# A fused recurrence and wave-MLP kernel: the same steps replayed in another order

## The chip, the core and the metric

The kernel runs on one core of a Trainium2 chip. A time is the device time of one execution in microseconds (us); lower is better. Five engines work side by side: TensorE (PE in the profile; its weight loads are listed as PEld), VectorE (DVE), ScalarE (ACT), GpSimd (POOL) and SyncE (SP), which here only issues transfers. Each engine takes its own instructions strictly in the order in which the program gives them, so an instruction that waits holds up all that stand behind it on that engine.

## The reference

Two stages in a row. The first is a linear recurrence over 768 tokens, for 4 batches and 8 heads of 64 columns:

```python
gamma = 1.0 - 2.0 ** (-5.0 - np.arange(H)); scale = 1.0 / np.sqrt(D)
for t in range(S):
    state = gamma[None, :, None, None] * state + einsum('bhd,bhe->bhde', k[:, :, t], v[:, :, t])
    y[:, :, t] = scale * einsum('bhd,bhde->bhe', q[:, :, t], state)
```

Its output, laid out as x of shape (4, 768, 512), goes through

```python
theta = x @ w_theta
zr, zi = x * np.cos(theta), x * np.sin(theta)
y = einsum('ts,bsd->btd', w_tok_r, zr) + einsum('ts,bsd->btd', w_tok_i, zi)
u = x + y
out = u + np.maximum(u @ w_ch, 0.0)
```

## The kernel before

The whole kernel is a set of small functions, one for each step, and a list of tokens, ORDER, which replays them: a token names a function and its arguments (`M.3.2` calls `M(3, 2)`), and a last letter p, v, a or s names the engine or the queue (POOL, DVE, ACT, SP). Nothing else schedules: ORDER is the program's order on every engine and on every transfer queue.

**The recurrence** is cut into 24 units: 4 batches, 3 stretches of 256 tokens, 2 halves of 4 heads. For unit n:

- `Lk`, `Lq`, `Lv` load 256 KB of k, q and v each, on the queue of SP or of ACT (tiles kqf and vf; 16 and 9 buffers). `ck`, `cq` or `cqs` and `cv` cast and scale them to bf16 (tiles kqb and vb).
- `Tk` and `Tq` transpose kqb on PE into kq_ps, and `E` copies that to kqT; for some units `Tk6`, `Tq6` and `E6` do so in 64-blocks, or `Dk` does it by a transposing transfer on SP's queue.
- `A` multiplies k by q (at_ps), `m` masks the product on DVE (at), `Y` multiplies by v into r_ps. `ST` makes the unit's contribution to the state, `S0` and `S1` add it up (s), `SB` casts the state (sbd), `I` multiplies it by q into r_ps.
- `XB` and `XA` bring r_ps to the transposed output xT of a 128-token tile C.

at_ps has one buffer: `A` of the next unit waits for `m`.

**The second stage** has 24 tiles of 128 tokens, six to a batch. `Hh` multiplies xT by w_theta (th_ps, four products of 512 columns), `CN` takes cosine and sine on ACT (cs), `Tx` and `Ex` or `Dx` bring x back to token rows (x_sb), `z` multiplies them (z). The two token matrices come in by `Pw` on POOL's queue (tile row; `Pth` and `Pch` bring wth and wch) and are transposed by `Tw` and copied by `Ew` (wtr, wti). `M(t, s0)` is two of the twelve 512-column products of output tile t (y_ps); `u` adds x on DVE; `Tu` and `Eu` or `Du` transpose; `O` is four products with w_ch (o_ps); `f` makes the output on DVE, and `SO` stores it. The last tile is done in halves (`Mh`, `uh`, `Oh`, `fh`, `SOh`).

th_ps, y_ps and o_ps share a pool of two banks, acc, which are given out in turn: a group that opens waits until the group two before it has been read, which is `CN` for th_ps, `u` for y_ps and `f` for o_ps. kq_ps, x_ps, w_ps and u_ps share two other banks in the same way.

`Z` issues two products of a zero tile whose result nobody reads; its number has no effect. `const1` clears the zero tile on DVE, `const2` makes positions and decays on POOL and arg on DVE, `const3` (ACT) the scales of q and v, `constA` (POOL), `const8` and `const9` (ACT) the decay table qx, `const4` the identity and `const5` the mask on POOL, `const6` clears sbd.

Of the kernel before, what the change touches and what calls it, by code (L numbers as in the profile page):

```python
# [24 lines left out]
cqs.1.p Tq.1 Lq.2.s S0.0.v SB.0.1.v A.0 Lk.2.s SB.0.0.p cv.1.p Lv.2.s S1.0 Z.15 I.0 Z.27 m.0 Tk.1 E.1.a  # L25
cqs.2.v Z.34 cv.2.p Y.0 ST.1 XB.0.1.a S0.1.v S1.1 SB.1.0.a Pth Lq.3.s Z.18 XB.0.0.v Tq.2 A.1 SB.1.1.a
ck.2.a I.1 m.1 Y.1 ST.2 Tk.2 const7 Z.23 XB.1.0.v Lk.3.s E.2.v XB.1.1.v A.2 ck.3.p S0.2.v m.2 S1.2
SB.2.1.a Z.11 cqs.3.p Tq.3 Lv.3.s Tx.0 Tk.3 Z.3 ck.4.p Lv.4.s Lk.5.s Lq.5.s Lv.5.s Lq.6.s Lk.6.s Lv.6.s
Lq.7.s E.3.a SB.2.0.v I.2 Y.2 XB.2.1.a Ex.0.a cv.3.v cq.4.p Tk.4 Lq.8.s A.3 ST.3 Lk.7.s S0.3.v SB.3.0.a
S1.3 Lv.7.s Lk.8.s Tx.1 Tq.4 SB.3.1.p cv.4.p m.3 Pw.1.0 XB.2.0.a Ex.1.a I.3 Lv.8.s E.4.a ck.5.a cq.5.a  # L30
Y.3 Pw.0.0 ST.4 Hh.0 S0.4.v XB.3.0.v XB.3.1.v cv.5.v CN.0.1 A.4 CN.0.0 Tq.5 Hh.1 Tk.5 SB.4.0.p SB.4.1.a
Pw.0.1 Hh.2 m.4 E.5.v I.4 Y.4 ST.5 ck.6.a Tk.6 Tx.2 cq.6.a CN.1.1 CN.1.0 XA.4.1 A.5 XA.4.0 m.5 Lq.9.s
Ex.2.v S0.5.v z.0.p Tq.6 E.6.a CN.2.0 cv.6.p Hh.3 SB.5.0.v Tx.3 Tw.1.0 z.1.v SB.5.1.a Ew.1.0.v Ex.3.a
CN.2.1 A.6 I.5 Y.5 ST.6 XA.5.0 z.2.v Tw.0.0 CN.3.0 Tx.4 CN.3.1 Ew.0.0.v S0.6.v XA.5.1 Ex.4.v Hh.4 CN.4.0
CN.4.1 Tw.0.1 M.0.1 Pw.1.1 z.3.v M.0.0 Tw.0.2 Pw.1.2 Ew.0.2.a SB.6.1.a Hh.5 z.4.p SB.6.0.p Lk.9.a M.0.3
ck.7.p cqs.7.p M.0.2 CN.5.1 CN.5.0 cq.8.v m.6 Ew.0.1.v Tw.1.1 Tw.1.2 Ew.1.1.v Lv.9.s M.0.4 M.1.0 Tx.5
Ew.1.2.v M.1.1 S1.6 Tk.7 M.1.4 Pch Ex.5.v z.5.v cv.7.v Tq.8 Tq.7 M.1.2 E.7.a M.0.5 I.6 Y.6 ST.7 A.7
ck.8.a u.0 S0.7.v m.7 XA.6.1 SB.7.1.a M.1.5 M.1.3 XA.6.0 Tw.1.3 M.2.5 Pw.0.2 M.2.3 u.1 S1.7 Tk.8 M.2.1
M.2.0 SB.7.0.v Ew.1.3.a Tu.0 I.7 cv.8.v E.8.a Lk.10.s cv.9.p Y.7 ST.8 A.8 cqs.9.v ck.9.v M.2.4 Du.1
Eu.0.a XB.7.1.a XB.7.0.v S0.8.v SB.8.0.v M.2.2 Tx.6 Tq.9 Tk.9 Lv.10.a ck.10.p cv.10.p Lq.10.s S1.8 u.2  # L40
m.8 O.0 E.9.a SB.8.1.a Hh.6 Tw.1.4 I.8 Y.8 A.9 CN.6.0 Du.2 Lq.14.s CN.6.1 Ex.6.v f.0 ST.9 Tw.0.3 Hh.7
Ew.1.4.v Ew.0.3.a S0.9.v Tw.0.4 M.3.0 CN.7.0 CN.7.1 M.3.2 Dx.7 M.3.1 M.3.5 M.3.3 Lv.11.s Lk.11.s XA.8.1
Ew.0.4.v Lq.11.s M.3.4 S1.9 u.3 Tw.0.5 Tk.10 M.4.5 cqs.10.p XA.8.0 m.9 M.4.3 Tq.10 SB.9.1.a SB.9.0.a I.9
O.2 Lq.12.s Lk.12.s E.10.a Lk.15.s Ew.0.5.v Lk.14.s Y.9 ST.10 Tw6.1.5 Ew6.1.5.0.a Ew6.1.5.1.a A.10 z.7.p
# [36 lines left out]
Du.18 O.19 M.21.0 M.21.3 M.20.2 Mh.1.2 Mh.1.0 Mh.1.4 u.22 O.18 Mh.1.3 SO.15.a f.19 M.20.0 M.20.1 Tuh.0
u.21 Du.22 Du.21 f.18 M.20.3 Euh.0 M.20.4 Mh.1.1 M.20.5 u.20 O.22 Mh.1.5 uh.1 f.22 Tu.20 SO.14.a SO.19.s
Eu.20.a O.21 SO.18.a Tuh.1 Euh.1 f.21 Oa.0 Oa.1 fa.0 fa.1 Oh.0 Oh.1 SO.21.a SO.22.s SO.20.s fh.0 SOh.0
fh.1 SOh.1 Z.31
""".split()


# [618 lines left out]
```

## Time and profile before

| | |
|---|---|
| time, median of 3 runs (lowest, highest) | 164.74 us (164.14, 164.97) |
| span of the profiled execution, first to last instruction | 163.3 us |
| PE busy | 154.7 us, 95% (2100 matmuls) |
| DVE busy | 114.5 us, 70% |
| ACT busy | 78.8 us, 48% |
| POOL busy | 74.3 us, 45% |
| moved by DMA | 35.19 MB, mean 215 GB/s |
| chain that ended last | PE 79%, DMA 7%, DVE 6%, POOL 4% |

The profile is one execution; its own time is not listed beside its span, and the median of the timed runs is 1.4 us longer than that span. Shares are over the whole span, which hides that the first 33 us differ from the rest: the views by stretch tell them apart. A matmul's busy time includes its passage through the array, so products that follow each other closely overlap in it; the distance between their starts is what they cost.

### The profile page before, as it was taken

To read this page: it belongs to the slowest core of one execution; us is meant where nothing else is said; L and a number is where in the kernel's file an instruction comes from. 1 tells how busy PE (TensorE), PEld (TensorE's weight loads), DVE (VectorE), ACT (ScalarE), POOL (GpSimd) and SP (SyncE) were. 2 spreads that over 40 slices of the span, in tenths; PEclk is the share of its full clock that TensorE was granted. 3 is DMA by queue.
4 is the path that set the end of the run, shared out by engine and by line. 5 is a ranking of instruction groups with operands and counts; after the bars stand their busy time and mean duration, and the time that the engine had idled before them with its cause. 6 is when DMAs were issued, how large, how long until landed. Compare 5 with 4: busy or idle time off the path is not lost.

```text
span 163.3 us, 5070 instructions
## 1 busy us (share of the span) xinstructions
PE 154.7 (95%) x2100; PEld 85.5 (52%) x2100; DVE 114.5 (70%) x217; ACT 78.8 (48%) x147; POOL 74.3 (45%) x106
## 2 busy tenths in 40 slices
PE   5996989999999998999999999999999999999992
PEld 1454646656666654644544655455545554444561
DVE  3388687987994786794999787698867760345362
ACT  4966698983658264673423645822341616000020
POOL 7657289176514770520057689910469204600000
PEclk9999999999999999999999999999999999999999
DMA  4999999999999999999999999999896527514446
GB/s 116 297 290 252 258 294 240 277 220 285 226 162 275 296 205 220 251 207 245 335 236 172 242 195 305 222 192 276 185 251 129 101 64 225 161 68 128 128 156 230
DMA packets 70118, 35.19 MB, mean 215 GB/s; under 512 B 27472, under 2 KB 67152, under 8 KB 70096
## 3 DMA queue, kind: packets, MB, share of 16 engines
q1 hardware_dynamic: 57088, 24.00, 68.6%
q10 hardware_dynamic: 10320, 7.47, 16.6%
q0 software_dynamic: 2688, 3.41, 12.1%
q8 instruction: 16, 0.26, 0.7%
q14 instruction: 6, 0.05, 0.1%
HBM read 25.69 MB, written 6.29 MB: 196 GB/s over the span
## 4 chain that ended last, share of the span: by engine, by line
PE 79%; DMA 7%; DVE 6%; POOL 4%; issue 1%; ACT 1%; DVEq 0%; POOLq 0%
PE y_ps L559 33%; PE o_ps L595 10%; PE th_ps L511 10%; PE zz L279 5%; PE r_ps L458 4%; PE at_ps L380 4%; DMA x_sb<-xT 4%; DMA kqT<-kqb 3%; PE kq_ps L318 3%; PE w_ps L533 2%; DVE at L389 2%; POOL z L525 2%; PE r_ps L446 2%; PE y_ps L620 2%; PE r_ps L408 1%
## 5 line engine op out<-in xcount | busy, mean ns | idle before, releaser
L559 PE MATMUL y_ps<-z,wtr 128*128 128x512 bf16 x138 | 52.4, 380 | 0.0
L559 PE MATMUL y_ps<-z,wti 128*128 128x512 bf16 x138 | 52.3, 379 | 0.0
L525 POOL TENSOR_TENSOR z<-cs,x_sb 128x1024 bf16<-128x1024 bf16 x12 | 25.5, 2135 | 17.7 <-ACT cs L518 10.8
L389 DVE TENSOR_TENSOR at<-at_ps,mask 128x1024 bf16<-128x1024 f32 x24 | 29.2, 1215 | 0.5 <-PE at_ps L380 0.5
L310 POOL TENSOR_TENSOR vb<-vf,vsc 128x512 bf16<-128x512 f32 x15 | 15.6, 1045 | 21.7 <-ACT sbd L136 11.7
L601 DVE SCALAR_TENSOR_TENSOR ot<-o_ps,u 128x512 f32<-128x512 f32 x22 | 15.1, 688 | 13.6 <-PE o_ps L595 13.5
L511 PE MATMUL th_ps<-wth,xT 128*128 128x512 bf16 x96 | 24.5, 380 | 0.0
L566 DVE TENSOR_TENSOR u<-y_ps,x_sb 128x512 bf16<-128x512 f32 x23 | 15.8, 688 | 10.9 <-PE y_ps L559 10.5
L595 PE MATMUL o_ps<-wch,uT 128*128 128x512 bf16 x88 | 22.6, 380 | 0.0
L518 ACT ACTIVATE cs<-th_ps,halfpi 128x512 bf16<-128x512 f32 x24 | 16.3, 682 | 11.8 <-PE th_ps L511 7.0
L518 ACT ACTIVATE cs<-th_ps,zerob 128x512 bf16<-128x512 f32 x24 | 16.4, 684 | 10.6 <-PE th_ps L511 5.1
L559 PEld LDWEIGHTS <-wtr 128*128 128x128 bf16 x138 | 13.5, 98 | 13.4
L559 PEld LDWEIGHTS <-wti 128*128 128x128 bf16 x138 | 13.5, 98 | 12.7 <-issue 0.4
L138 POOL CAST sbd<-s 64x256 bf16<-64x256 f32 (+1 forms) x20 | 8.4, 418 | 24.3 <-DVE s L426 22.1
L136 ACT COPY kqT<-kq_ps 128x1024 bf16<-128x1024 bf16 (+1 forms) x10 | 9.7, 969 | 9.8 <-PE kq_ps L318 9.5
L511 PEld LDWEIGHTS <-xT 128*128 128x128 bf16 x96 | 8.7, 98 | 8.5
L279 PE MATMUL zz<-zero 128*128 128x512 bf16 x30 | 10.8, 495 | 1.9 <-DVE zero L191 1.9
L595 PEld LDWEIGHTS <-uT 128*128 128x128 bf16 x88 | 8.1, 98 | 8.4 <-issue 0.2
L136 ACT CAST kqb<-kqf 128x512 bf16<-128x512 f32 x16 | 9.6, 620 | 5.5 <-DMA kqf<-in_k_dram 5.4
L458 PE MATMUL r_ps<-at,vb 64*64 64x128 bf16 x384 | 10.0, 221 | 1.6 <-DVE at L389 1.6
L380 PE MATMUL at_ps<-kqT 64*64 64x128 bf16 x384 | 10.0, 220 | 1.1 <-DVE kqT L138 0.6
L476 DVE TENSOR_TENSOR xT<-r_ps,qx 128x256 bf16<-128x256 f32 x22 | 8.7, 417 | 1.8 <-PE r_ps L458 0.8
(88 smaller groups left out, 209.4 us busy)
## 6 DMA issues: line engine op xcount, KB each, us to landing
vf<-in_v_dram SPq DMA_DIRECT2D x20, 256.0 KB, 5.7
kqf<-in_k_dram SPq DMA_DIRECT2D x19, 256.0 KB, 5.4
kqf<-in_q_dram SPq DMA_DIRECT2D x17, 256.0 KB, 5.7
out_dram<-ot ACTq DMA_DIRECT2D x12, 256.0 KB, 2.5
out_dram<-ot SPq DMA_DIRECT2D x11, 256.0 KB, 2.4
kqf<-in_q_dram ACTq DMA_DIRECT2D x7, 256.0 KB, 5.4
kqf<-in_k_dram ACTq DMA_DIRECT2D x5, 256.0 KB, 6.7
vf<-in_v_dram ACTq DMA_DIRECT2D x4, 256.0 KB, 5.7
```

Source lines behind the costliest of these rows:

```text
L136: nc.scalar.copy(dst, src)
L279: nc.tensor.matmul(t[:m, :cols], K["zero"][:, :m], K["zero"][:, :cols], start=True, stop=True)
L310: engines[e].tensor_mul(in_blocks(vb), by_token(raw["vf", n]), _bcast_last(K["vsc"][:, i, :, h * HU:(h + 1) * HU], D))
L380: nc.tensor.matmul(at_ps[cols, g, j, a, :], kq_at(n, 0, a, j, c)[rows], kq_at(n, 1, slice(0, 2), j, c)[rows], start=(j == 0 and a == 0), s ...
L389: nc.vector.tensor_mul(at.rearrange("p g j a t -> p (g j) (a t)"), st["at_ps", n].rearrange("p g j a t -> p (g j) (a t)"), _bcast_mid(K["m ...
L458: nc.tensor.matmul(st["R", n + 1][c][g * D:(g + 1) * D, j * P:(j + 1) * P], st["vb", n][rows, lo:lo + D], st["at", n][rows, g, j, a, :], s ...
L511: nc.tensor.matmul(th_ps, st["xT", C][:, j, :], K["wth"][:, j, :], start=(j == 0), stop=(j == 3))
L518: nc.scalar.activation(st["cs", C][:, w, :], st["th_ps", C], AF.Sin, bias=K["zerob" if w else "halfpi"], scale=1.0)
L525: engines[e].tensor_mul(st["z", b][:, c], st["cs", C], _bcast_mid(x_of(C), 2))
L559: nc.tensor.matmul(st["y", t], K["wT"][r][:, s0, t0 * P:(t0 + 1) * P], st["z", b][:, s0, r, :], start=(done == 0 and r == 0), stop=(done = ...
L566: nc.vector.tensor_add(st["u", t], st["y", t], st["x", b][:, t0, :])
L595: nc.tensor.matmul(o_ps, st["uT", t][:, j, :], K["wch"][:, j, :], start=(j == 0), stop=(j == nD - 1))
```

## The change

Only ORDER is replaced, one table of tokens by another. Nearly all its lines differ, so the diff says little by itself; its first and last lines are

```diff
-const2 Lv.0.s const1 const6.v Z.29 Z.2 const5 Z.38 Lk.0.a const3 Z.35 Z.8 Lq.0.s Lv.1.s Z.28 constA
-const4 Lq.1.a const9 Lk.1.s Z.39 const8 ck.0.p Tk.0 ck.1.a cqs.0.v cv.0.v Tq.0 E.0.v Lq.4.a ST.0 Lk.4.a
...
+const1 Lq.1.a Z.472 const6.v Z.617 Lv.0.s constA Z.838 const2 const4 Lk.1.s Lk.0.a Z.896 Lq.0.s const3
+Z.362 cqs.1.v Lv.1.s ck.0.p Tk.0 const9 cv.0.v ck.1.p Z.692 ST.0 Lq.4.a cqs.0.v S0.0.a Tq.1 S1.0 Tq.0
...
-fh.1 SOh.1 Z.31
+Euh.1 Oa.1 fa.0 Oh.0 Oh.1 fa.1 SO.21.s fh.0 SO.20.s fh.1 SOh.0 SOh.1 Z.31
```

Of the 936 tokens before, 928 are left: the eight that go are `Z`, of which 15 become 7 (30 zero products become 14). Before, seven stand ahead of `Tk.0`, seven among units 0 to 3, one at the end; now five ahead of `Tk.0`, one behind it, one at the end. All other steps are there once as before. Another engine has 128 of the casts, copies and scalings, and 9 of the stores another queue (four from ACT's to SP's, five the other way). The rest is order. As the file is one line shorter, line numbers in the rows of the changed kernel are smaller by one.

Place 1, ACT at the very start. kqf is a load; qsc and vsc are `const3`; qx of 512 columns is `const9` and of 256 is `const8`; kqT<-kq_ps is `E`; s<-r_ps is `S0`; the cast kqb<-kqf is `ck.1`. Before:

```order
L156 DMA kqf<-in_k_dram 128x4x128
L239 ACT_TABLE_LOAD
L239 ACTIVATE qsc<-arg,lscale 128x48
L239 ACTIVATE vsc<-arg,zerob 128x48
L156 DMA kqf<-in_q_dram 128x4x128
L232 ACTIVATE qx<-pos,lscale,lgp 128x512 x4
L232 ACTIVATE qx<-pos,lscale,lgp 128x256 x4
L136 CAST kqb<-kqf 128x512
L156 DMA kqf<-in_q_dram 128x4x128
L156 DMA kqf<-in_k_dram 128x4x128
L136 COPY kqT<-kq_ps 128x1024
```

Now:

```order
L155 DMA kqf<-in_q_dram 128x4x128
L155 DMA kqf<-in_k_dram 128x4x128
L238 ACT_TABLE_LOAD
L238 ACTIVATE qsc<-arg,lscale 128x48
L238 ACTIVATE vsc<-arg,zerob 128x48
L231 ACTIVATE qx<-pos,lscale,lgp 128x512 x4
L155 DMA kqf<-in_q_dram 128x4x128
L135 COPY s_199<-r_ps 128x128
L155 DMA kqf<-in_k_dram 128x4x128
L135 COPY kqT<-kq_ps 128x1024
L231 ACTIVATE qx<-pos,lscale,lgp 128x256 x4
```

The k of unit 0 is now the second load of ACT's queue. The copy to kqT is now that of unit 0 (before, of unit 1; unit 0 had it on DVE), behind the large half of the qx table and two loads, and ahead of the small half.

Place 2, POOL at the start, from the positions on. pos and lgp are `constA`, posn to zerob `const2`, mask `const5`, kqb `ck`, the sbd casts `SB`. Before:

```order
L204 IOTA posn 128x6
L208 MEMSET lg 128x1 x8
L210 MEMSET lscale 128x1
L212 MEMSET halfpi 128x1
L214 MEMSET zerob 128x1
L260 MEMSET mask 128x256
L264 AFFINE_SELECT mask<-mask 64x128 x4
L222 IOTA pos 128x768
L227 MEMSET lgp 64x1 x8
masks.py:197 MEMSET ident 128x128
masks.py:199 AFFINE_SELECT ident<-ident 128x128
L138 CAST kqb<-kqf 128x512
```

Now, from the positions of `const2` on (pos and lgp stand ahead of these rows):

```order
L203 IOTA posn 128x6
L207 MEMSET lg 128x1 x8
L209 MEMSET lscale 128x1
L211 MEMSET halfpi 128x1
L213 MEMSET zerob 128x1
masks.py:197 MEMSET ident 128x128
masks.py:199 AFFINE_SELECT ident<-ident 128x128
L137 CAST kqb<-kqf 128x512 x2
L137 CAST sbd_74<-s_199 64x2x64
L259 MEMSET mask 128x256
L263 AFFINE_SELECT mask<-mask 64x128 x4
L137 CAST sbd_74<-s_199 64x2x64
```

The mask has moved from the front to behind two casts and an `SB`, which waits for unit 0's state; pos and lgp have moved ahead of what arg needs.

Place 3, PE at the end of output tile 8, where the th_ps group of tile 13 opens (`M` of tile 8, then `Hh.13`). With buffer numbers; y_ps_1976 and y_ps_1869 are tile 8's bank. Before:

```order
L559 LDWEIGHTS wtr_101
L559 MATMUL y_ps_1976<-z_1427,wtr_101 128x512
L559 LDWEIGHTS wti_102
L559 MATMUL y_ps_1976<-z_1427,wti_102 128x512
L511 LDWEIGHTS xT_1972
L511 MATMUL th_ps_2064<-wth_99,xT_1972 128x512
```

Now:

```order
L558 LDWEIGHTS wtr_80
L558 MATMUL y_ps_1869<-z_1458,wtr_80 128x512
L558 LDWEIGHTS wti_81
L558 MATMUL y_ps_1869<-z_1458,wti_81 128x512
L510 LDWEIGHTS xT_1945
L510 MATMUL th_ps_2029<-wth_78,xT_1945 128x512
```

The rows look alike, but the bank differs. Before, tile 8 opened its bank after `O.5`, so `Hh.13` takes the bank of `O.5`, and the one that takes tile 8's is the group behind it, that of `M.10.1`. Now tile 8 opens before `O.5`, so `Hh.13` itself takes tile 8's bank and waits for `u.8`.

More of the change, by code (lines that the diff above doesn't have):

```diff
@@ L28 @@
[L28 to L32, printed above, removed]
@@ new lines @@
+M.11.4 M.11.1 SB.17.0.a Lk.19.s ck.22.v SB.17.1.a CN.15.1 XA.16.0 M.11.2 ck.21.v XA.16.1 m.17 CN.15.0
+I.17 Hh.14 u.11 Y.17 Ex.15.a z.12.p ST.18 Eu6.8.0.v CN.14.0 XA.17.1 S0.18.a XA.17.0 CN.14.1 S1.18
+SB.18.1.p Dx.14 Tu6.11 A.18 SB.18.0.a z.15.v O.10 ck.19.a Eu6.11.1.v Eu6.11.0.a z.14.p Hh.17 f.10
+CN.17.1 Tq.19 Lq.23.s m.18 I.18 SO.7.s Tk.19 CN.17.0 cv.19.p O.8 E.19.v Hh.16 SO.1.s CN.16.1 f.8 Lq.22.a
+A.19 Tx6.17 Y.18 ST.19 Lv.23.s O.11 CN.16.0 M.13.0 Ex6.17.1.a Dx.16 M.13.2 z.16.p m.19 M.13.3 f.11
@@ L85 @@
+Euh.0 O.22 Mh.1.4 SO.18.a SO.19.a Tu.20 f.22 Mh.1.3 Mh.1.5 O.21 SO.22.s Eu.20.a uh.1 Tuh.1 Oa.0 f.21
+Euh.1 Oa.1 fa.0 Oh.0 Oh.1 fa.1 SO.21.s fh.0 SO.20.s fh.1 SOh.0 SOh.1 Z.31
 """.split()
```

106 lines of the change are left out of this document (52 added, 54 removed).

## The prediction

> **What bounds the kernel now.** I read the page first, for the engine that has no room.
>
> ```profile
> span 163.3 us, 5070 instructions
> PE 154.7 (95%) x2100; PEld 85.5 (52%) x2100; DVE 114.5 (70%) x217; ACT 78.8 (48%) x147; POOL 74.3 (45%) x106
> PE   5996989999999998999999999999999999999992
> DMA  4999999999999999999999999999896527514446
> ```
>
> PE is busy for 95% of the span. Busy is no proof of full use, so next come the stretches, cut at the first th_ps product, the first y_ps product and the last one of the kernel (us, then busy time and count of PE, PEld, DVE, ACT, POOL, the granted clock, the DMA share and GB/s).
>
> ```profile
> 7.82:22.15 14.33, 11.49 (x275) 7.79 (x274) 10.74 (x21) 9.88 (x20) 8.41 (x12) 1.00 1.19 271
> 22.15:32.70 10.55, 10.31 (x183) 6.54 (x179) 9.13 (x19) 9.68 (x18) 6.31 (x8) 1.00 1.17 266
> 32.70:64.00 31.30, 31.30 (x423) 18.45 (x420) 24.96 (x49) 18.61 (x32) 16.98 (x16) 1.00 1.16 237
> 64.00:104.00 40.00, 39.35 (x682) 21.39 (x682) 32.87 (x60) 19.74 (x44) 20.66 (x22) 1.00 1.19 247
> 104.00:159.80 55.80, 55.80 (x534) 29.12 (x533) 33.29 (x60) 15.17 (x29) 16.66 (x17) 1.00 0.69 159
> 159.80:163.30 3.50, 0.58 (x4) 0.08 (x1) 0.60 (x2) 0.00 (x0) 0.00 (x0) 1.00 0.61 217
> ```
>
> From 32.70 to 159.80, that is 127.1 us, PE sits idle for 0.65 us (the 64 to 104 row: 40.00 less 39.35). Those products all stay. So the time is the moment of the first y_ps product, plus 127.1, plus whatever PE waits more or less than 0.65 us in between, plus a tail of 3.5 us. The order can win in the first 32.7 us, where PE is idle by 2.84 us and 0.24 us in two rows and also computes zeros, and it can lose anywhere.
>
> The 0.65 us has two places, from the timeline:
>
> ```profile
> 64.90 0.42 PE L380 MATMUL at_ps<-kqT 64*64 64x128 bf16 x16 [0.49 <-DMA kqT<-kqb]
> 103.05 0.45 PE L318 MATMUL kq_ps<-ident,kqb 128*128 128x128 bf16 x5 [0.16 <-POOL kqb L138]
> ```
>
> **The head, part by part.** The rows of the timeline on which the walk rests (start, duration, what; in brackets the engine's idle time ahead and who ended it):
>
> ```profile
> 1.38 0.21 DVE L216 TENSOR_TENSOR arg<-posn,lg 128x48 f32<-128x48 f32 x1 [1.38 <-POOL lscale L210]
> 1.59 0.27 DVE L191 MEMSET zero<- 128x256 uint32 x1
> 1.67 1.28 ACT L239 ACT_TABLE_LOAD   x1 [1.67 <-DVE arg L216]
> 1.92 6.06 PE L279 MATMUL zz<-zero 128*128 128x512 bf16 x14 [1.92 <-DVE zero L191]
> 2.96 0.78 POOL L222 IOTA pos<- 128x768 f32 x1
> 3.68 1.07 POOL L227 MEMSET lgp<- 64x1 f32 x8
> 3.96 4.89 ACT L232 ACTIVATE qx<-pos,lscale,lgp 128x512 f32<-128x512 f32 x8 [0.43 <-POOL lgp L227]
> 5.33 0.61 POOL L138 CAST kqb<-kqf 128x512 bf16<-128x512 f32 x1
> 6.07 0.69 DVE L304 TENSOR_TENSOR kqb<-kqf,qsc 128x512 bf16<-128x512 f32 x1 [3.11 <-DMA kqf<-in_q_dram]
> 7.18 1.08 POOL L304 TENSOR_TENSOR kqb<-kqf,qsc 128x512 bf16<-128x512 f32 x1 [1.24 <-DMA kqf<-in_q_dram]
> 7.82 0.61 PE L318 MATMUL kq_ps<-ident,kqb 128*128 128x128 bf16 x8
> 8.46 0.69 DVE L138 COPY kqT<-kq_ps 128x1024 bf16<-128x1024 bf16 x1 [1.10 <-PE kq_ps L318]
> 9.18 0.53 ACTq L156 DMA_DIRECT2D kqf<-in_k_dram  x1
> 9.21 0.42 PE L380 MATMUL at_ps<-kqT 64*64 64x128 bf16 x16 [0.21 <-DVE kqT L138]
> 10.97 1.01 ACT L136 COPY kqT<-kq_ps 128x1024 bf16<-128x1024 bf16 x1 [1.61 <-PE kq_ps L318]
> ```
>
> *Zero products.* Of the chain of waits, one row gives their later price, and the fourteen first ones above give the early one, 6.06/14 = 0.43 us each:
>
> ```profile
> 10.28 0.43 PE zz L279 x2
> ```
>
> So each is 0.43 us at first and 0.216 us later. The zero tile's clearing no longer waits behind arg, so they start some 0.5 us earlier, near 1.3, and ten of them end near 5.6. The six pairs that go from units 0 to 3 were 6 x 0.43 = 2.6 us of PE; they stood where the next real step was late anyway, so by themselves I cost them at nothing, and what they hid is walked through next.
>
> *Unit 0.* The second load of a kind that was asked for lands about 6.0 (the scaling at 6.07 starts on it) and the fourth about 7.1 (the one at 7.18). k of unit 0 is now second on its queue, so it lands between these, its cast of 0.61 follows, and the first transpose stands near 7.2, against 7.82. Then it loses: arg waits for pos and lgp, 1.8 us of POOL, so the table load starts near 3.6, the scales end near 5.4, the large half of qx (four of eight in 4.89 us, the longer ones, some 2.9) ends near 8.3. Behind it come a load (0.5), the state copy, another load (0.53) and only then unit 0's kqT, at 1.01 on ACT against 0.69 on DVE: done near 10.5, where it was done at 9.15. The product of k and q follows, 1.3 us later than at 9.21. The mask, now behind an `SB` on POOL, is done near 11.1 and no later than that product.
>
> *Units 1 to 5.* The mask products are the beat of this stretch:
>
> ```profile
> 13.00 1.22 DVE L389 TENSOR_TENSOR at<-at_ps,mask 128x1024 bf16<-128x1024 f32 x1
> 20.41 1.21 DVE L389 TENSOR_TENSOR at<-at_ps,mask 128x1024 bf16<-128x1024 f32 x1
> 26.99 0.42 PE L380 MATMUL at_ps<-kqT 64*64 64x128 bf16 x16
> 29.07 0.50 PE L533 MATMUL w_ps<-ident,row 128*128 128x128 bf16 x6
> 32.70 0.38 PE L559 MATMUL y_ps<-z,wtr 128*128 128x512 bf16 x1
> ```
>
> I walked the new order by hand with these durations, each step starting at the last of its inputs and of its engine. `E.1` now stands on DVE behind `m.0`, so `m.1` is at 13.5 (13.00 before). `ck.2` and `SB.1.0` stand on ACT behind the small half of qx, which delays `Y.1` by 1.3 us, but `Tk.2` and `Tk.3` stand ahead of `Y.1` now and not behind it, so `E.2` runs during the wait: `m.3` near 21.0 (20.41). There `Hh.0` and `Hh.1`, 1.7 us of real products, stand ahead of `Y.3` and fill its wait. Unit 5's product of k and q comes near 26.4 (26.99), and the first y_ps product near 32.1 (32.70): **-0.6 us**. The error of such a walk is some 1 us on either side; the bounds for the first y_ps product are 31.0, if `E.0` and the loads come at the early end, and 33.6.
>
> *Casts elsewhere.* By means from the costliest groups, kept apart by shape:
>
> ```profile
> L136 ACT COPY kqT<-kq_ps 128x1024 bf16<-128x1024 bf16 x9 | 9.1, 1011 | 9.5 <-PE kq_ps L318 9.5
> L138 DVE COPY kqT<-kq_ps 128x1024 bf16<-128x1024 bf16 x3 | 2.1, 688 | 1.2 <-PE kq_ps L318 1.1
> ```
>
> Net five such copies go from ACT to DVE: +3.4 us there and -5.1 here. Counting all 128 with the means of their groups, DVE gains about 1 us, ACT loses 4, POOL gains 0.5. After 32.70 PE hides that: DVE has 36 us of room there. Without that cover the price would be DVE's 1 us. Cost: nothing.
>
> **The middle.** Here I looked for places where PE's next step has too little PE work ahead of it to cover its chain. One stands out, place 3: `Hh.13` takes the bank of tile 8 and waits for `u.8`, straight behind tile 8's last product. The trace has the same pair, with `Hh.13` between:
>
> ```profile
> 85.75 0.38 PE L559 MATMUL y_ps<-z,wti 128*128 128x512 bf16 x1
> 85.96 1.03 PE L511 MATMUL th_ps<-wth,xT 128*128 128x512 bf16 x4
> 86.16 0.69 DVE L566 TENSOR_TENSOR u<-y_ps,x_sb 128x512 bf16<-128x512 f32 x1 [0.24 <-PE y_ps L559]
> 86.91 0.38 PE L559 MATMUL y_ps<-z,wtr 128*128 128x512 bf16 x1
> ```
>
> From 85.96, when PE was free of tile 8, to 86.91, when the bank was, is 0.95 us; now it is a hole: **+0.95 us** (0.9 to 1.3, as DVE has `f.5`, `S0.14` and `XA.13.1` just ahead). Queued behind it on PE are `A.15` and tile 10.
>
> The two old holes should close: unit 11's kqT transfer was issued late because its k cast stood on POOL behind a z of 2.1 us, and now stands ahead of it; the other hole was the k cast of unit 19 on POOL, which moves to ACT. **-0.65 us** (0 to -0.65).
>
> Other banks with under 0.3 us to spare (`M.14` on `u.13`, `M.18` on `f.16`), the late z of the last batch, and SP's queue, where `Du.17` stands behind `Dx.22` and `Du.15`: **+0.1 us** (0 to 0.6). The stores: the last tile's half store stands behind one more store on SP, which has its data earlier: nothing (0 to 0.3).
>
> **The sum:** -0.6 + 0.95 - 0.65 + 0.1 = -0.2 us, from a span of 163.3 to 163.1. The median of the runs is 1.44 us above that span, so 164.5 us. What a measurement of this kernel can tell from no change is about 0.5%, 0.8 us; the forecast is no change, or a little faster.
>
> **Rivals.**
>
> *The head wins more (faster, 163.0).* If my walk of unit 0 is late by the 1.3 us of kqT, the reordering of `Tk.2`, `Hh.0` and `Hh.1` pays in full and the first y_ps product stands at 31.0 to 31.2: -1.6 in place of -0.6 and, with `u.8` fully paid, 163.5; with no small waits and an early start of the first transpose at 6.7, 163.0. For it: 2.6 us of zeros are gone, and DVE and ACT have less ahead of that point. Against: the waits of this stretch are chains of copies, not PE. It decides from a first y_ps product before 31.5.
>
> *The cold PE (slower, 166.2).* The fourteen first zero products run at half the speed of the later ones, and the speed changes near 7.4, after 5.5 us of unbroken work. Now there are only 4.3 us of it, then a gap to 7.2 and no zeros later. If half speed lasts to the middle of the 7.82 to 22.15 stretch, whose real products take some 8 us at full speed, PE needs 4 us more there, and as it waits much of that time anyway, I take somewhat under half: +1.7. Against: real work also counts as work. The point from which it decides is full speed reached after 11 us. The Trainium skill, "TensorE: Matmul & The Clock Gate", section "What's actually happening", says that PE starts at half clock and is released only after a busy window of about 3.4 us, which runs freely, and falls back after an idle one. The trace agrees with the half speed and needed 5.5 us. By that rule ten zero products are sure to fill one window in about a quarter of the phases, an estimate from the page's window.
>
> *The weights come late (slower, 165.4).* `Pw.1.0` now stands on POOL behind another scaling, near 23.0 where it was issued at 21.67, and took 5.7 us to land:
>
> ```profile
> row<-in_moe_w_tok_i_dram POOLq DMA_DIRECT2D x1, 192.0 KB, 5.7
> ```
>
> It would land at 28.7, and its first transpose (29.07 before) is due near 28.1: +0.6, and +0.9 if the transfer takes a little longer, as DMA is full here.
>
> **Chances.** The forecast 0.37, of which 0.02 lies beyond the bound on the faster side; the head wins more 0.34; the cold PE 0.18; late weights, or a wait of that size that I haven't seen, 0.11, of which 0.02 stays within the bound. So faster 0.36, same 0.37, slower 0.27. The forecast's own range is 163.8 to 165.4; the range that holds 8 in 10 goes from 162.6 (the first y_ps product at its early bound) to 166.6 (the cold PE with the small waits).
>
> **What would show it.** Right: ten zero products ending before 6, kqT of unit 0 on ACT near 9.5 to 10.5, the first y_ps product near 32, an idle PE of about 1 us ahead of th_ps behind a `u`, and none at 65 and 103. Wrong: PE products of one shape twice as far apart at 9 us as at 20 us (the cold PE), a w_ps that waits for row, DVE waiting for v of unit 7, or any hole over 0.5 us after the first y_ps product that is not `Hh.13`.

## The result and the profile after

The changed kernel is slower: median 170.24 us of four runs (169.03 to 174.77) against 164.48 us; the ratio is 1.033, 95% interval 1.028 to 1.039. Ratios here and below leave out disturbed executions, such as that of 174.77, and medians do not, so a ratio can be smaller than the quotient of the medians. The profiled execution took 169.03 us with a span of 167.3.

The page of the changed kernel: its head, the busy tenths of PE, the clock that PE was granted in tenths of full speed, and the chain that ended last:

```profile
span 167.3 us, 5046 instructions
PE 153.1 (92%) x2084; PEld 84.5 (51%) x2084; DVE 118.0 (71%) x217; ACT 74.5 (45%) x144; POOL 74.6 (45%) x109
PE   6559699899999999999899999996999998999993
PEclk9955999999999999999999999999999999999999
PE 49%; DMA 24%; DVE 11%; issue 5%; SPq 4%; POOL 4%; ACT 1%; DVEq 0%; ACTq 0%; POOLq 0%
```

The chain was 79% PE before; now half of it runs through transfers, DVE and the queues. Here are the stretches of the changed kernel, cut at its own first transpose, first th_ps product, first y_ps product and last zero pair (columns as in the prediction; a granted clock of 1.00 is full speed, 0.50 is half):

```profile
7.61:20.85 13.24, 9.93 (x235) 7.27 (x236) 8.95 (x17) 8.93 (x20) 11.53 (x20) 0.74 1.20 275
20.85:32.54 11.69, 10.68 (x206) 6.83 (x206) 9.89 (x19) 10.26 (x21) 7.94 (x10) 1.00 1.17 278
32.54:64.00 31.46, 31.20 (x419) 18.34 (x417) 26.56 (x49) 16.02 (x29) 15.22 (x18) 1.00 1.20 237
64.00:104.00 40.00, 39.10 (x682) 21.23 (x681) 32.17 (x64) 21.21 (x45) 17.05 (x20) 1.00 1.19 236
104.00:163.79 59.79, 57.15 (x541) 29.40 (x539) 36.93 (x64) 13.93 (x27) 19.53 (x16) 1.00 0.66 152
163.79:167.30 3.51, 0.59 (x4) 0.09 (x1) 0.61 (x2) 0.00 (x0) 0.00 (x0) 1.00 0.60 212
```

The first y_ps product is at 32.54 (32.70 before) and the tail is 3.51 (3.50). The middle, from the one to the other, is 131.25 us and was 127.1: all the loss is there, and most of it behind 104 us, where PE idles 2.64 us and idled none before. These are PE's rows behind an idle time of over 0.15 us from the first y_ps product on:

```profile
35.88 0.51 PE L532 MATMUL w_ps<-ident,row 128*128 128x128 bf16 x6 [0.23 <-DMA row<-in_moe_w_tok_i_dram]
82.23 0.27 PE L445 MATMUL r_ps<-kqT,sbd 128*128 128x128 bf16 x2 [0.64 <-ACT xT L135]
85.26 0.32 PE L407 MATMUL r_ps<-vb,kqb 64*64 64x64 bf16 x16 [0.26 <-DVE vb L309]
115.14 0.42 PE L379 MATMUL at_ps<-kqT 64*64 64x128 bf16 x16 [1.56 <-DMA kqT<-kqb]
121.50 0.38 PE L558 MATMUL y_ps<-z,wtr 128*128 128x512 bf16 x1 [0.36 <-DVE u L565]
123.98 0.38 PE L445 MATMUL r_ps<-kqT,sbd 128*128 128x128 bf16 x4 [0.16 <-DVE xT L475]
141.88 1.04 PE L594 MATMUL o_ps<-wch,uT 128*128 128x512 bf16 x4 [0.55 <-DMA uT<-u]
```

Only the waits at 121.50 and 123.98 have a cause in common. Measured by the distance of the starts less the usual distance, they cost a little more than they idle: `A.20` (115.14) 1.63, `I.13` (82.23) 0.75, `O.17` (141.88) 0.71, the products behind `Hh.18` (121.50) 0.54, `ST.14` 0.32, `I.21` 0.32, the place at 35 us 0.40, one at `A.15` 0.17: 4.84 us together. The middle without any wait is 127.1 - 0.65 = 126.4, and 131.25 less that is 4.8, so the list is complete for this execution. It is not the same in every execution. Four of the waits, 3.20 of the 4.84 us, stand in all five profiled executions whose rest keeps this order (this one and g3, g4, z2 and h2 below): `A.20`, the products behind `Hh.18`, `I.21` and `O.17`. The others come and go: the wait of `I.13` is 0.64 us here, 0.17 in g3, 1.77 in z2, and absent in g4 and h2, and the places between 35 and 50 us differ each time. Two of the four can be followed back in the rows.

`A.20` waits for a transposing transfer, `Dk.20`. ACT's timeline and SP's, each in the changed kernel:

```profile
109.55 0.37 ACT L135 CAST xT<-r_ps 128x256 bf16<-128x256 f32 x1 [1.78 <-DVE s L429]
109.82 0.62 ACT L135 CAST kqb<-kqf 128x512 bf16<-128x512 f32 x1
```

```profile
110.46 1.42 SPq L366 DMA_TRANSPOSE kqT<-kqb  x1
```

The q cast of unit 20 (109.82) was on POOL before; now it stands on ACT behind `XB.18.1` (109.55), for which ACT stood idle for 1.78 us. The transfer is issued the moment the cast ends, lands 4.6 us later, and `A.20` starts at 115.14. The cast of 0.62 us had been counted as moved at no cost; what it cost is the wait of its neighbour.

The products behind `Hh.18` wait for `u.14`. DVE's timeline, and POOL's:

```profile
119.31 1.53 DVE L303 TENSOR_TENSOR kqb<-kqf,qsc 128x512 bf16<-128x512 f32 x1
120.77 0.68 DVE L565 TENSOR_TENSOR u<-y_ps,x_sb 128x512 bf16<-128x512 f32 x1
```

```profile
118.86 1.43 POOL L309 TENSOR_TENSOR vb<-vf,vsc 128x512 bf16<-128x512 f32 x1 [4.94 <-DMA vf<-in_v_dram]
120.25 1.07 POOL L137 CAST kqb<-kqf 128x512 bf16<-128x512 f32 x1
```

The scaling of q of unit 23 came to DVE from POOL, ahead of `u.14`, and takes 1.53 us there, where the other three of this kernel on DVE take 0.69, 0.85 and 1.09. POOL works at the same moment, and its two steps are long as well (1.43 for 1.04, 1.07 for 0.61).

### The profile page after: what moved, and what is told of

Same layout as the page of the kernel before. It is cut to its first block, busy times and chain, and to the rows that moved or that the text cites. A ratio compares the mean times of both kernels' runs of the same rounds, so it can differ in the third digit from the quotient of the medians.

```text
span 167.3 us, 5046 instructions
## 1 busy us (share of the span) xinstructions
PE 153.1 (92%) x2084; PEld 84.5 (51%) x2084; DVE 118.0 (71%) x217; ACT 74.5 (45%) x144; POOL 74.6 (45%) x109
## 4 chain that ended last, share of the span: by engine, by line
PE 49%; DMA 24%; DVE 11%; issue 5%; SPq 4%; POOL 4%; ACT 1%; DVEq 0%; ACTq 0%; POOLq 0%
PE y_ps L558 21%; PE o_ps L594 10%; PE th_ps L510 5%; DMA row<-in_moe_w_tok_i_dram 5%; DMA kqf<-in_q_dram 5%; DMA vf<-in_v_dram 4%; DMA kqf<-in_k_dram 3%; DMA x_sb<-xT 3%; DMA kqT<-kqb 3%; PE at_ps L379 2%; PE r_ps L457 2%; DVE z L524 2%; DMA uT<-u 2%; SPq L155 2%; PE w_ps L532 2%
## 5 line engine op out<-in xcount | busy, mean ns | idle before, releaser
L524 POOL TENSOR_TENSOR z<-cs,x_sb 128x1024 bf16<-128x1024 bf16 x11 | 23.7, 2158 | 14.8 <-DMA x_sb<-xT 10.4
L309 POOL TENSOR_TENSOR vb<-vf,vsc 128x512 bf16<-128x512 f32 x13 | 14.3, 1101 | 10.5 <-DMA vf<-in_v_dram 10.2
L137 POOL CAST kqb<-kqf 128x512 bf16<-128x512 f32 x15 | 10.1, 679 | 12.5 <-DMA kqf<-in_k_dram 9.3
L303 POOL TENSOR_TENSOR kqb<-kqf,qsc 128x512 bf16<-128x512 f32 x9 | 9.4, 1043 | 8.5 <-DMA kqf<-in_q_dram 8.4
L379 PE MATMUL at_ps<-kqT 64*64 64x128 bf16 x384 | 11.0, 227 | 2.3 <-DMA kqT<-kqb 1.6
L524 DVE TENSOR_TENSOR z<-cs,x_sb 128x1024 bf16<-128x1024 bf16 x13 | 10.6, 817 | 2.7 <-ACT cs L517 2.5
L135 ACT CAST sbd<-s 64x256 bf16<-64x256 f32 (+1 forms) x20 | 7.4, 371 | 10.6 <-DVE s L425 8.4
L135 ACT CAST xT<-r_ps 128x256 bf16<-128x256 f32 x18 | 6.5, 370 | 12.1 <-DVE s L425 6.3
```

Source lines behind the costliest of these rows:

```text
L135: nc.scalar.copy(dst, src)
L137: engines[e].tensor_copy(dst, src)
L309: engines[e].tensor_mul(in_blocks(vb), by_token(raw["vf", n]), _bcast_last(K["vsc"][:, i, :, h * HU:(h + 1) * HU], D))
L379: nc.tensor.matmul(at_ps[cols, g, j, a, :], kq_at(n, 0, a, j, c)[rows], kq_at(n, 1, slice(0, 2), j, c)[rows], start=(j == 0 and a == 0), s ...
L524: engines[e].tensor_mul(st["z", b][:, c], st["cs", C], _bcast_mid(x_of(C), 2))
```

## The experiments

Theory W: the loss is a sum of single late inputs behind the first y_ps product. Rivals: H, it comes from the head; C, the missing zero products and the clock; S, slack is so short everywhere that a mended place only hands its wait on; and the question whether order or engines do it.

### Head or rest

Two tables were spliced: new up to the first y_ps product and old from there, and the reverse.

```diff
 h1: new table up to M.0.1, then the old table's remaining steps (its later Z left out)
 h2: old table up to M.0.1, then the new table's remaining steps (its last Z left out)
```

> The new table up to its first y_ps product (nine zero products' tokens fewer, new order and engines of units 0 to 5), then every step that is left in the order and on the engines of the old table. Theory M (the loss is a sum of late inputs behind the first y_ps product; the head is worth -0.2): 164.3, between 163.5 and 165.2. Theory H (the loss comes from the head: fewer zero products and a colder PE, or loads that slide from there): 168 to 170.

Measured: 172.62 us, ratio 1.049 (1.042 to 1.055), above what either theory said, and for a reason of the seam. DVE's and PE's timeline of this kernel, and its windows:

```profile
39.16 0.43 DVE L135 CAST kqb<-kqf 128x512 bf16<-128x512 f32 x1 [5.60 <-DMA kqf<-in_q_dram]
```

```profile
41.24 0.37 PE L530 MATMUL w_ps<-ident,row 128*128 128x128 bf16 x2 [4.92 <-DVE wtr L135]
```

```profile
36.32:41.24 4.92, 0.00 (x1) 0.00 (x0) 2.08 (x4) 0.00 (x0) 2.82 (x4) 0.82 1.15 258
41.24:46.00 4.76, 4.76 (x22) 2.62 (x22) 2.85 (x6) 0.00 (x0) 1.04 (x1) 0.50 1.18 218
```

The old rest casts q of unit 8 early on DVE; the new head loads k of unit 8 first. One load in the wrong place held DVE for 5.6 us and PE for 4.9, and then the granted clock was 0.50 for another 4.8 us.

> The mirror: the old table up to its first y_ps product with all its zero products, the rest of the steps in the new order on the new engines. Theory M: 169 to 170.5, as the changed kernel. Theory H: 164 to 165.

Measured: 170.76 us, ratio 1.035 (1.027 to 1.043), as theory M has it. The first y_ps product is at 32.30 and the middle 131.6 us, and behind 104 us the waits are the same ones (1.43, 0.36, 0.17 and 0.56 us). The last stretch of h2, to lay beside that of the changed kernel:

```profile
104.00:163.90 59.90, 57.38 (x545) 29.57 (x542) 36.79 (x64) 14.12 (x27) 19.93 (x16) 1.00 0.65 152
```

The seam of h1 was mended by exchanging two loads:

```diff
-Lk.8.s ... Lq.8.s
+Lq.8.s ... Lk.8.s
```

> The new head with the old rest once more, with the loads of q and k of unit 8 exchanged, so that the q, which the old rest casts at 34 us on DVE, is loaded first as in the old table. In the first such kernel DVE waited 5.6 us for that load (landed at 39.07), PE 4.9 us for DVE, and then ran five products pairs at half clock. Theory M (the new head is worth -0.2 us): 164.6, between 163.8 and 165.5. Theory H (the new head costs several us): over 167.

The profiled execution took 164.19 us with a span of 162.5 and a middle of 126.3, with no wait of PE over 0.2 us. The other runs took 166.66 to 170.08, so no ratio can be given and this kernel alone decides nothing. Their mean granted clocks were 0.97 to 1.00, against 0.97 in the short one, so the clock does not explain them. z4 below says more.

### Order or engines

```diff
 h3: the new order; -cq.20.a +cq.20.p, and so for all 128 steps and 9 stores: the old letters
 h4: the old order; -cq.20.p +cq.20.a, and so on: the new letters
```

> The new order, every step on the engine or queue that it had before. Theory O (the order by itself makes the late inputs, above all on PE, SP and DVE): 168.5 to 170.5. Theory L (the 128 steps on another engine make them: a cast behind a waiting instruction, as the q cast of unit 20 on ACT): 164.5 to 166. A third one, T (order and engines fit each other, and each table is spoiled by the other's engines): over 170.5.

> The old order, with the engine or queue of every step as in the new table. Theory O: 164.5 to 166. Theory L: 168.5 to 170.5. Theory T: over 167, and over 170.5 if the fit is worth more than the order.

Measured: h3 178.15 us, ratio 1.082 (1.076 to 1.087); h4 192.43 us, 1.166 (1.158 to 1.174). Neither theory O nor L, but T, for both: which engine does a cast and where it stands are one decision. So the change can't be split into an order's part and an engines' part, and a price for the casts on other engines by themselves means nothing here.

### Single late inputs

```diff
 f1
-cq.20.a (behind XB.18.1.a)      +cq.20.a (ahead of Ex6.17.1.a)
-cqs.23.v                        +cqs.23.p
 k2: the second line alone
```

> The changed kernel with two steps moved: the q cast of unit 20 stays on ACT but stands ahead of Ex6.17.1 and so ahead of XB.18.1, behind which it waited; the scaling of q of unit 23 (1.53 us on DVE, ahead of u.14) goes back to POOL, which idles there. Theory W (the loss is the sum of single late inputs, each with its own place): the 1.63 us ahead of A.20 go, and the 0.54 and 0.32 us behind u.14 and SB.21.0, so -2.4 us: about 167.2. Rival S (the shortest slack goes from one place to the next: with these inputs early, another input is late within a few us and takes the time back): 169 to 170, with new waits of PE between 110 and 130 us.

Measured: 167.74 us, ratio 1.017 (1.011 to 1.023), where the changed kernel has 1.033. No row of PE waits for `u.14`, and that of `A.20` has no idle time ahead of it:

```profile
114.36 0.39 PE L377 MATMUL at_ps<-kqT 64*64 64x128 bf16 x16
```

Its middle is 130.1 us. The wait of `I.21` is still 0.17 us, now behind POOL, and that of `O.17` stays. Near 38 and 40 us this execution has two waits, 0.64 and 0.57, that the changed kernel's first execution lacks; they are no price of the two moves, since g3, the changed kernel again, has the like (0.41 and 0.57).

> The changed kernel with the scaling of q of unit 23 back on POOL and nothing else. Theory W: the waits of 0.36 and 0.16 us behind u.14 and SB.21 go and about 0.9 us with them, 169.2 beside 170.1; the 1.6 us ahead of A.20 stay. Rival S: no change.

Measured: 168.15 us, ratio 1.021 (1.014 to 1.029). In DVE's timeline `u.14` starts at 119.26 (120.77 in the changed kernel), while in PE's the wait for `Dk.20` stays:

```profile
115.09 0.42 PE L377 MATMUL at_ps<-kqT 64*64 64x128 bf16 x16 [1.26 <-DMA kqT<-kqb]
```

The middle is 130.5 us (131.25 in the changed kernel, 131.8 when it was run again as g3). So one scaling moved to DVE costs about 1 us here. That size is rough: k2's interval touches the changed kernel's, and its execution also lacks the wait of `I.13`, which comes ahead of the move. The pair of moves in f1 gives back half of the loss, with intervals that lie apart: theory W for these places.

```diff
 f2
-O.17 Mh.0.4 O.16 ... f.17 z.23.p f.16      +O.16 Mh.0.4 O.17 ... f.16 z.23.p f.17
-Lk.18.a XB.12.1.a                          +XB.12.1.a Lk.18.a
-Lk.21.s ... Lq.16.s ... Lq.17.s ... Lv.14.s  +Lv.14.s Lk.21.s ... Lq.16.s ... Lq.17.s
```

> The changed kernel with three places mended: O.16, whose uT has landed, ahead of O.17 (0.71 us of wait); XB.12.1 on ACT ahead of Lk.18, a load whose issue waited there for another transfer to land (0.75 us ahead of I.13); Lv.14 on SP ahead of Lk.21, Lq.16 and Lq.17, which are needed much later (0.32 us ahead of ST.14, and more once I.13 comes early). Theory W: -1.8 us, about 167.8. Rival S: 169 to 170, and new waits of PE at 82 to 90 us or behind 140 us.

Measured: 170.56 us, ratio 1.032 (1.027 to 1.038): nothing gained. The three waits are gone from its trace, and two new ones make up for them. PE's timeline of f2, and SP's:

```profile
96.02 1.04 PE L592 MATMUL o_ps<-wch,uT 128*128 128x512 bf16 x3 [1.46 <-DMA uT<-u]
147.30 0.27 PE L617 MATMUL y_ps<-z,wtr 128*128 128x256 bf16 x1 [0.59 <-POOL z L522]
```

```profile
89.34 2.30 SPq L501 DMA_TRANSPOSE x_sb<-xT  x1
91.69 1.27 SPq L587 DMA_TRANSPOSE uT<-u  x1
```

In the changed kernel the first of these two, `Dx.13`, was issued 1.15 us earlier, at 88.19, and in 1.20 us, and `Du.7` behind it went at 89.43; here `Dx.13` takes 2.30 and `Du.7` goes at 91.69. Of the 1.15 us, 0.54 is the later course of this whole execution (`Hh.13` is at 86.92 against 86.38). The second wait is rival S: `O.17` no longer waits, and the product on z of tile 23 does, in f2 and again in f3 and z3. The first is not settled: f3, which has f2's order up to here, has no wait at `O.7`, and its `Dx.13` took 1.77. SP issues here without a pause, so a longer issue makes the next thing late; why the issue differs between executions stays open.

> The changed kernel with both sets of moves. Theory W: the parts add up, -4.2 us, 165.4 (164.8 to 166.3), that is the kernel before with a little more. Rival S: 167.5 to 169.5.

Measured, f1 and f2 together: 166.52 us, ratio 1.010 (1.006 to 1.013), between the two expectations. The interval overlaps f1's a little, so what f2's moves add is less sure than what f1's do. Of the 3.3% some 2.3 are regained. The middle is 128.8 us; PE's rows show waits that were not there before:

```profile
96.54 0.42 PE L377 MATMUL at_ps<-kqT 64*64 64x128 bf16 x16 [0.41 <-DMA kqT<-kqb]
142.18 0.27 PE L617 MATMUL y_ps<-z,wtr 128*128 128x256 bf16 x1 [0.58 <-POOL z L522]
```

Two kernels tried to take the rest.

```diff
 g1: f3, with z3's eight pairs of zero products (below), and
-Dx.13.. Du.7 .. Dk.17     +Dk.17 straight behind Dk.16
-z.23.p                    +z.23.v
-Tw.1.1 M.0.0 M.0.4        +M.0.0 M.0.4 Tw.1.1
-cv.7.v Lq.9.s z.5.v       +Lq.9.s z.5.v cv.7.v
 k1: f3, with the same zero products, z.23.v, and Lk.22 moved behind Dk.17
```

> The changed kernel with the four moves of before, the eight pairs of zero products, and four places more: Dk.17 on SP straight behind Dk.16 (0.67 us of wait ahead of A.17); z.23 on DVE, which idles there, and not on POOL (0.86); the weight transpose Tw.1.1 two pairs of products later (0.47); cv.7 on DVE behind z.5, which then runs clear of POOL's cv.8 (0.49). Theory W: another -2.5 us from 164.8 of span, 162.4 to 163.2, so 164.0 to 165. Rival S: 166 to 168, with new waits of PE.

Measured: 173.67 us, ratio 1.057 (1.049 to 1.064). The profiled execution is the shortest of its four (170.06 us; the others 173.38 to 175.54), and one wait stands out in it. SP's timeline of g1, PE's, and the windows around the wait:

```profile
84.54 5.30 SPq L364 DMA_TRANSPOSE kqT<-kqb  x2
91.82 1.27 SPq L587 DMA_TRANSPOSE uT<-u  x1
```

```profile
96.63 1.89 PE L592 MATMUL o_ps<-wch,uT 128*128 128x512 bf16 x4 [3.24 <-DMA uT<-u]
```

```profile
93.39:96.63 3.24, 0.01 (x1) 0.00 (x1) 1.90 (x5) 0.94 (x3) 1.68 (x1) 0.99 1.23 209
96.63:100.00 3.37, 3.37 (x8) 1.16 (x9) 0.69 (x1) 0.00 (x0) 2.94 (x3) 0.50 0.47 93
```

The issue of `Dk.17`, put first, took some 3 us, `Du.7` went 2.4 us later than in the changed kernel, PE stood for 3.24 us, and half clock followed. That this move makes the loss is read from the trace; no run has it alone, and what made the other runs 3.3 to 5.5 us longer still isn't shown.

> The changed kernel with the four moves, the eight pairs of zero products, z.23 on DVE (0.86 us of wait ahead of its product) and the load Lk.22 on SP behind Dk.17 and not ahead of it (0.57 us earlier for Dx.13, Du.7 and Dk.17; PE waited 0.67 us for Dk.17). Theory W: 163.3 of span, 164.5 to 165.5, ratio 1.000 to 1.006. Rival S (what is won at one place is lost at the next): 166.5 or more.

Measured: 167.15 us, ratio 1.013 (1.003 to 1.023), no better than f3. Its profiled execution is its longest (170.50) and isn't read here. So the last 1% stays open: these attempts won nothing over f3, and no run shows a version of the new order that is as fast as the old one.

### The zero products

```diff
 z1, the old table: -Z.28 -Z.39 -Z.27 -Z.34 -Z.18 -Z.23 -Z.11 -Z.3
 z2, the new table: +Z +Z behind Z.362, +Z +Z behind Tk.1, +Z behind each of I.0, Tq.2, Tx.0, I.2
 z3: f3 with the Z of z2        z4: f4 with the Z of z2
 g3: the changed kernel again   g4: z2 again, both in one session with 5 rounds
```

> The kernel before without eight of its fifteen pairs of zero products: the last two of the opening seven pairs and six later ones, so five pairs at the start, one behind the first state steps and the last one stay. Nothing else. Theory C (the zero products keep the clock up; without them PE is halved for some us in the first 20 and the time gets longer and varies from run to run): 165 to 167.5, runs over a range of 2 us or more. Rival N (they are filler beside transfers): 164.0 to 164.8 and a range under 1 us, as the kernel before.

Measured: 167.21 us (runs from 165.05 to 168.97), ratio 1.008 (1.003 to 1.013). The median is 1.6% above the 164.50 of the kernel before beside it. This is theory C, in size as well: with nothing else changed, the first y_ps product moves from 32.70 to 33.80 and the middle stays at 127.1. The range of the runs tells less than was expected, as the kernel before itself ran from 163.79 to 165.85. The stretch of z1 that the prediction showed with a clock of 1.00:

```profile
7.82:22.15 14.33, 11.07 (x213) 8.15 (x214) 9.67 (x21) 8.72 (x18) 7.26 (x11) 0.64 1.20 270
```

> The changed kernel with eight pairs of zero products more, put where its PE waits in the head: two at the end of the opening, two ahead of A.0, and one each behind I.0, Tq.2, Tx.0 and I.2. Theory C: the granted clock stays at 1.0, a range of the runs under 1 us, and 168 to 169 (the late inputs behind the first y_ps product stay). Rival N: as the changed kernel, 169 to 171 and a range of 1.5 us or more.

> The changed kernel once more, as a yardstick beside the next one: 169 to 170.5.

> The changed kernel with eight pairs of zero products more in its head, beside the changed kernel on the same chip. Theory C (half clock in the head costs time here too): 0.8 to 1.5 us less than the changed kernel beside it. Rival N: within 0.5 us of it, since PE waits for its inputs at the first y_ps product anyway.

Measured: z2 169.31 us, ratio 1.029 (1.022 to 1.036). Side by side, g3 has 170.07 us, 1.032 (1.027 to 1.038), and g4 169.56 us, 1.027 (1.021 to 1.033). The mean granted clock of g3's runs is 0.97 to 0.98 and that of g4's profiled run 1.0; the first y_ps product comes at 32.82 and 32.43. So 0.4 to 0.5 us of a loss of 5.4 look like the clock's. That is less than theory C's 0.8 and at the bound of rival N's 0.5. The intervals overlap, so the size isn't settled, but it is a small part; one run of the changed kernel had a mean clock of 0.998 and took 169.69 us all the same. All the kernels with the new head bear it out: the first y_ps product comes at 31.80 to 33.07 us in eight profiled executions without the pairs (mean 32.55), and at 31.59 to 32.43 in six with them (mean 32.00).

> The changed kernel with all the moves for its late inputs and the same eight pairs of zero products. Theory C: 164.8 to 165.6 with a range under 1 us. Rival N: 165.8 to 167, as without the pairs.

Measured: 167.57 us, ratio 1.017 (1.009 to 1.024). Here the pairs brought no gain over f3; neither theory is supported.

> The new head with the old rest, q of unit 8 loaded first, and the eight pairs of zero products in the head. Without them one execution had a span of 162.5 and no wait of PE over 0.2 us behind the first y_ps product, and others were 2.5 to 6 us longer. Theory C: 163.4 to 164.4 with a range under 1 us. Rival N: a median near 167 and a range of several us; then something else than the clock varies.

Measured: 164.48 us, ratio 0.998 (0.995 to 1.002). With the clock full, the new head with the old rest is as fast as the kernel before in eight of ten runs; the other two took 167.18 and 167.30 with a clock of 0.997 and 1.00, so something else lengthened them. PE hardly idles behind 64 us, 0.16 us in all:

```profile
64.00:104.00 40.00, 39.84 (x686) 21.64 (x685) 32.74 (x61) 20.35 (x45) 21.31 (x22) 1.00 1.17 249
104.00:159.30 55.30, 55.30 (x530) 28.84 (x528) 33.37 (x60) 14.57 (x28) 16.12 (x17) 1.00 0.75 158
```

With h2 this settles head or rest for the changed kernel: the new rest carries the loss under either head, and the new head with its eight pairs does not lose under the old rest. What the new head does there without the pairs stays open, by the spread of f4.

### The old order with its two waits mended

```diff
 g2, the old table with two moves
-XB.9.1.a XB.9.0.a f.2 M.4.0 O.1 M.4.1 cq.11.a   +cq.11.a XB.9.1.a XB.9.0.a f.2 M.4.0 O.1 M.4.1
-ck.21.p ck.19.p                                +ck.19.p ck.21.p
```

> The kernel before with cq.11 on ACT ahead of XB.9.1 (so that the transposing transfer of unit 11 is issued 0.6 us earlier; PE waited 0.49 us for it) and ck.19 on POOL ahead of ck.21 (PE waited 0.16 us for it). Theory W: -0.65 us, 163.9, ratio 0.996. Rival S: 1.000 to 1.005, another input is late.

Measured: 164.37 us against 164.66, ratio 0.997 (0.994 to 0.9998). Both old waits are gone, and PE has not a hundredth of idle time from the first y_ps product on:

```profile
32.78:64.00 31.22, 31.22 (x423) 18.52 (x420) 25.08 (x49) 18.62 (x32) 16.55 (x16) 1.00 1.23 228
64.00:104.00 40.00, 40.00 (x686) 21.74 (x686) 33.24 (x61) 20.49 (x45) 21.43 (x22) 1.00 1.22 260
104.00:158.78 54.78, 54.78 (x529) 28.69 (x527) 32.80 (x60) 14.31 (x28) 15.90 (x17) 1.00 0.68 158
```

That was all the idle time there was behind the head, and it is worth 0.3%, barely clear of noise. Both moves are within one engine.

## Why the prediction was wrong

- **What bounds the kernel: right.** The time did come out as first y_ps product plus middle plus tail, and the tail (3.51) was right.
- **The head, -0.6: -0.16 measured, and the sign isn't shown.** Executions of the new head differ by more than that (31.80 to 33.07 for the first y_ps product; the kernel before and the two others with its whole head, h2 and g2, 32.30 to 32.78). The walk held at its start: zero products to 5.7 (5.6 said), first transpose 7.61 (7.2), the copy to kqT done at 10.29 (10.5). For the 0.4 us that are missing at the end (32.54; 32.1 said) there are two causes that the runs don't separate: the clock (0.39 between g3 and g4), and a wait for the token matrix just ahead of the first y_ps product. PE's row of the changed kernel:

```profile
31.97 0.51 PE L532 MATMUL w_ps<-ident,row 128*128 128x128 bf16 x6 [0.71 <-DMA row<-in_moe_w_tok_r_dram]
```

- **`Hh.13` on `u.8`, +0.95: wrong.** The step that failed is "takes the bank of tile 8"; the wait is not there. PE's and DVE's rows of the changed kernel:

```profile
86.38 1.03 PE L510 MATMUL th_ps<-wth,xT 128*128 128x512 bf16 x4
```

```profile
85.12 0.68 DVE L600 SCALAR_TENSOR_TENSOR ot<-o_ps,u 128x512 f32<-128x512 f32 x1
86.58 0.69 DVE L565 TENSOR_TENSOR u<-y_ps,x_sb 128x512 bf16<-128x512 f32 x1 [0.25 <-PE y_ps L558]
```

`Hh.13` starts at 86.38, before `u.8` has begun to read tile 8, so it is not in that bank; the other one had been free since `f.5` ended at 85.8. That the two banks are given out strictly in turn, as the description of the kernel and place 3 have it, is not so: in ORDER `f.5` stands ahead of `u.8`, which fits that the bank read first is given out first.
- **The old waits close, -0.65: right in size, for unit 11 by luck**; no PE row waits at 65 or 103 us. The reason given for unit 11, a k cast on POOL behind z, is wrong: that cast ended at 57.26. The last input was the q cast on ACT, behind two `XB`, which ended at 59.32; the transfer went at 59.39. ACT's timeline of the kernel before:

```profile
58.67 0.65 ACT L136 CAST kqb<-kqf 128x512 bf16<-128x512 f32 x1
```

g2 moves that cast ahead of the two `XB`, and the wait is gone; so the old order could have had this gain alone.
- **"Other banks ... and SP's queue: +0.1 us (0 to 0.6)": this is the step that lost the forecast.** It should have been +4.8. With it, -0.16 + 0 - 0.65 + 4.84 gives +4.0 us, and the span went from 163.3 to 167.3. The prediction had set as a sign of being wrong any hole over 0.5 us that is not `Hh.13`, and three came (1.56, 0.64 and 0.55). `Du.17` behind `Dx.22` and `Du.15` was named and costed at next to nothing; it costs 0.71. `A.20` (1.63) was not seen: the search names banks, the late z and SP's queue, and not the inputs of each transposing transfer: who makes them now, and behind what.
- **"Casts elsewhere": "Cost: nothing", as DVE has 36 us of room: wrong.** The sums for ACT and POOL were right (ACT 74.5 us busy, 4.3 less; POOL 0.3 more), but DVE gained 3.5 us (118.0) and not 1. And room over 127 us is no room at one place: k2 prices one such scaling at about 1 us, and h3 and h4 show what wrong places cost.
- **The stores: nothing, right** as far as the tail shows.
- **The rival of the cold PE: its condition came, its price didn't.** The clock was half until 16 us, past the point of 11 us that was set; the price was 0.4 to 0.5 us and not 1.7. In the old order (z1) it was 1.1 to 1.4. Adding zero products did lift the clock: from 7.6 to 20.9 us it was 0.74 in g3 and 1.00 in g4. The Trainium skill, "TensorE: Matmul & The Clock Gate", section "What's actually happening", says that activity releases the throttle and that an idle window of about 3.4 us brings it back. The trace of h1 agrees (half clock behind 4.92 us of idle time), and that of g1 nearly (behind 3.24). The changed kernel's own head does not: there half clock came behind 1.90 us (last section), and the measurement decides.
- **The rival of the late weights: its wait came, inside the head.** In 13 of the 14 executions with the new head a w_ps product waits 0.41 to 1.29 us for a `row` ahead of the first y_ps product: in g3 1.29 at 29.34, for `Pw.1.0` as described; in the changed kernel's first execution 0.71 at 31.97, for another of the loads. None of the four with the old head has it. The price wasn't its own +0.6, since the first y_ps product came no later than before.
- **The chances.** A wait "of that size that I haven't seen" had 0.11 together with the weights. With most of the order new and PE 99.5% busy behind the head, there was at most 0.65 us to win there and many places to lose; that asymmetry should have set the odds.

## What to carry over

When a kernel's bound engine is already busy without a gap, any reordering of the others can only lose there; cost it by walking the inputs of each thing that engine waits for (above all transfers that are issued by another engine's finished cast), not by totals per engine. A step moved to an idle engine costs the wait of whatever stands ahead of it there. Look at a second execution of the same order before a wait is put down to the order. Products that compute nothing can be worth their place if they keep the clock up; take them out alone, and look at the granted clock.

## What the runs showed of the hardware

- Issuing a transposing transfer keeps SP for 1.19 to 2.87 us (median 1.24, 38 of them, in the changed kernel), against a median of 0.57 us for its other transfers. From 84 to 94 us SP issues almost without a pause, and with one such issue put first PE waited 3.24 us (g1).
- A scaling on DVE that reads two operands of the on-chip buffer took 1.53 us beside POOL's work, against 0.69 at its shortest. The Trainium skill, "SBUF — State Buffer", section "Who interferes with whom", says that the one of the two engines that issues second is then blocked until the other is done. The rows agree roughly: POOL's step ended at 120.29 and DVE's at 120.84, 0.55 later, which is a little under the 0.69.
- The half clock comes back within the kernel, and not only at its start: 0.50 over 4.76 us behind 4.92 us without work (h1), and 0.50 over 3.37 us behind 3.24 us (g1). Products at half clock take twice their time (a zero product 0.43 us against 0.216), so these stretches cost some 2.4 and 1.7 us more, half as much again as the waits (an estimate from these figures).
- In the changed kernel's head the half clock came back with PE idle for much less. PE's timeline there, and windows of 2 us:

```profile
7.61 0.40 PE L317 MATMUL kq_ps<-ident,kqb 128*128 128x128 bf16 x4 [1.90 <-POOL kqb L137]
```

```profile
6.00:8.00 2.00, 0.39 (x5) 0.34 (x6) 0.66 (x2) 2.00 (x4) 1.06 (x2) 1.00 1.22 290
8.00:10.00 2.00, 1.61 (x31) 0.93 (x28) 0.94 (x2) 1.14 (x3) 0.98 (x5) 0.79 1.22 291
14.00:16.00 2.00, 1.82 (x28) 1.24 (x30) 1.58 (x3) 1.98 (x5) 1.86 (x4) 0.50 1.24 284
16.00:18.00 2.00, 1.36 (x54) 1.03 (x47) 1.33 (x4) 1.73 (x5) 1.58 (x4) 1.00 1.21 185
```

The clock was full by 6 us, PE idled 1.90 us and then worked, and from some point between 8 and 10 us until 16 the clock was half. It differs between executions of the same head: in f4 it was half from some point between 8 and 10 us to one between 18 and 20.
